# Two output projections in one slot, an earlier PSUM evacuation, and two low parts on GpSimd, in a fused attention and MLP block

## The chip, the cores and the metric

The kernel runs on one core of a Trainium2 chip. The metric is the device time of the program in microseconds (us). Times of a kernel are given as the median of several runs; the profile shows one execution, taken by the hardware profiler. The engines are called PE (TensorE; PEld its weight loads), DVE (VectorE), ACT (ScalarE), POOL (GpSimd) and SP (SyncE, which issues nearly all DMAs).

## The reference

A transformer block in float32 over 2048 rows of width 512. All the computing is in these lines:

```python
# attention on LayerNorm(x): 32 heads of 16, window of 8 positions with stride 2
qkv = layernorm(x) @ wqkv                      # 512 x 1536
logits = einsum("bhsd,bhswd->bhsw", q, k[idx]) * 16**-0.5   # idx = pos - 2*(0..7), masked below 0
o = einsum("bhsw,bhswd->bhsd", softmax(logits), v[idx])
h = x + o @ wo                                 # 512 x 512
# MLP on LayerNorm(h): 1792 hidden units, squared ReLU
r = relu(layernorm(h) @ w1 + b1)
out = h + (r * r) @ w2 + b2
```

## The kernel before

**Tiles.** The 2048 rows are 16 tiles of 128 rows, t = 0 to 15, and a block is R = 4 tiles (512 rows). Each matrix product keeps close to float32 precision by splitting each operand into a high part (a cast, `hi`, L152, always on ACT) and a low part (the difference, `lo`, L155, on DVE or POOL), and by summing three products: high by high, high by low, low by high. For one 128x512 result over a depth of 512 this is 12 matmuls (`mm3`, L228).

**Stages.** First the projections to q, k and v, whose results go through DRAM; then passages u = 0, 1, 2 (the text counts them 1, 2, 3), and then a last passage (4) of another form. The windowed attention (products on DVE at L340 and L351, sums on DVE at L374 and on POOL at L408) runs as a stream of steps beside all of it: `pump` emits as many of its DVE steps as a running estimate of PE's and DVE's time lets in.

**A passage u** has FB + LAG = 17 slots p = 0 to 16 and does three things at once on PE:

- `mlp1(u, f)` in slots 0 to 13: the first product of the MLP of block u, for hidden block f (128 hidden units x 512 rows), 12 matmuls into a PSUM bank. Its evacuation `hidden` (on ACT: bias and ReLU at L875, square at L876, cast to the high part `rh`; then the low part `rl` on POOL) is put with `at(1, ...)`, so it is emitted in the next slot.
- `mlp2(u, f)` in slots 3 to 16, three slots behind: the second product (L899), into four `acc` banks.
- For the four tiles t = 4(u + 1) + i of the next block: `wo_product` (attention output times `wo`, 12 matmuls into a bank), in the slots of the table `WP`: 9, 10, 13, 14 for passages 1 and 2. Behind it `h_add` (DVE adds `x` and takes the LayerNorm statistics), `h_norm` (three small POOL instructions for the factor, then ACT at L196), `add_b2` on POOL and `spill` (a store of `h` to DRAM), each so many slots after the product as the tuple in the call says.

**Turning.** An operand of a product must lie with its depth on the partitions, so o and the normalised h have to be transposed. Most tiles go through the DMA: ACT splits the float32 words into two 16-bit planes (`turn_split`, L621), SP issues a transposing DMA (`turn_dma`, L625), ACT joins the planes (`turn_join`, L630), and then high and low parts are made (`o_join`: `oh`, `ol`, or `ohl` for the third tile of a block; `h_parts`: into `big_l`, which also holds `hh` and `hl`, the operands of mlp1). The third and fourth tile of blocks 1 and 2 turn their h on PE instead (`h_T`, L201), in slot 16, ahead of and in the middle of that slot's second product.

**Order inside a slot.** `at(d, ...)` puts work into the list `due` of the slot d further on, `after` into `late`, `midway` into `amid`. A slot emits first the chores of its table entry (with `wo_product` last among them), then mlp1, then mlp2, and at its end `due`, the attention steps of `pump`, `amid` and `late`. Each engine runs its own instructions in the order in which they were emitted, and waits at the first one that is not ready. PE, ACT, DVE, POOL and SP are five such queues.

**Banks.** In the passages `turn["mm"]` and `turn["tr"]` are one turn over two banks, `mm1` and `mm0`: each mlp1, each `wo_product` and each `h_T` takes the other bank than the one before it in program order. It can be written only when the engine that reads its last content is done.

**The last passage** computes block 3's first product by a scheme with seven instead of eight quarter products. Its operands are sums of quarters of `hh`, made by `split_last` for tiles 12 to 15: for tiles 14 and 15 ACT casts, DVE forms the sums `s` (L757, L758, L766, L767), and low parts go into `big_l` (`hl` and `a_l[2]`) and `wo_l` (`a_l[1]`, `a_l[3]`, `a_l[4]`). `products_a` (L822) begins the passage on PE with the quarter products 1, 6, 5, 4; number 5 reads `a_h[1]` and `a_l[1]`, number 4 reads the third and fourth tile's part of `hh` and `hl`.

Of the kernel before, what the change touches and what calls it, by code (L numbers as in the profile page):

```python
# [19 lines left out]
R = 4  # L20
# [23 lines left out]
W2 = (18,)  # L44
LH = 3, 4, 10, 11
OP = 6, 7, 12, 13
WP = 9, 10, 13, 14
HP = 15, 15, 16, 16
UP = 14, 14, 15, 15
HL = (13, 0), (13, 1), (15, 0), (15, 1)  # L50
# [8 lines left out]
def block_kernel(ctx, tc, x, wqkv, wo, w1, b1, w2, b2, out):  # L59
    nc = tc.nc  # L60
# [52 lines left out]
    def at(delta, fn, *a):  # L113
        due.setdefault(now["slot"] + delta, []).append((fn, a))

    def after(delta, fn, *a):
        late.setdefault(now["slot"] + delta, []).append((fn, a))
# [33 lines left out]
    def hi(dst, src):  # L151
        nc.scalar.copy(dst, src)  # L152

    def lo(eng, dst, src, h):
        eng.tensor_tensor(out=dst, in0=src, in1=h, op=ALU.subtract)  # L155
# [53 lines left out]
    def hi_T(tr, h_dst):  # L209
        for d, src in parts(tr, h_dst):  # L210
            hi(d, src)
# [525 lines left out]
    def split_last(i, tr):  # L737
        hs_, ls_ = [a[:, :, i] for a in hh], [a[:, :, i] for a in hl]
        if i < RI:
            hi_T(tr, hs_)  # L740
            lo_T(tr, hs_, ls_)
            return
        j = i - RI
        tr0 = last_tr[j]
        if not j:
            a_h.update({2: hh[0][:, :, RI:], **{m: wo_h[:, m % 4].rearrange(
                "p (k i c) -> p k i c", k=2, i=RI) for m in (1, 3, 4)}})
            a_l.update({2: hl[0][:, :, RI:], **{m: wo_l[:, m % 4].rearrange(
                "p (k i c) -> p k i c", k=2, i=RI) for m in (1, 3, 4)}})
            for m in range(1, 5):  # L750
                s32[m] = row("s").rearrange("p (k i c) -> p k i c", k=2, i=RI)
        sm = {m: s32[m][:, :, j] for m in (1, 2)}
        sub, add = ALU.subtract, ALU.add
        tt = nc.vector.tensor_tensor
        a21 = tr[:, :2]
        hi(hs_[1], tr[:, 2:])
        tt(out=sm[1], in0=tr[:, 2:], in1=a21, op=add)  # L757
        tt(out=sm[2], in0=sm[1], in1=tr0[:, :2], op=sub)  # L758
        lo(nc.vector, ls_[1], tr[:, 2:], hs_[1])
        hi(a_h[2][:, :, j], sm[2])  # L760
        lo(nc.vector, a_l[2][:, :, j], sm[2], a_h[2][:, :, j])
        if not j:
            return
        hi(a_h[1], s32[1])
        for j in range(RI):
            tt(out=s32[3][:, :, j], in0=last_tr[j][:, :2], in1=last_tr[RI + j][:, :2], op=sub)  # L766
            tt(out=s32[4][:, :, j], in0=last_tr[j][:, 2:], in1=s32[2][:, :, j], op=sub)  # L767
        for m in (3, 4):
            hi(a_h[m], s32[m])
        for m in (1, 3):  # L770
            lo(nc.vector, a_l[m], s32[m], a_h[m])
# [97 lines left out]

    hid = {}  # L870

    def hidden(u, f, ps):
        r = row("r")
        rh, rl = work.tile([P, D], F32R, name="rh", bufs=LAG + 1), row("rl", dt=F32R)
        nc.scalar.activation(r, ps, AF.Relu, bias=b1_sb[:, f:f + 1])  # L875
        nc.scalar.activation(r, r, AF.Square)  # L876
        hi(rh, r)
        at(0, lo, nc.vector if u == R - 1 else nc.gpsimd, rl, r, rh)
        hid[u, f] = rh, rl

    def mlp1(u, f):
        ps = turn["mm"].tile("mm")
        fs = slice(f * P, (f + 1) * P)
        mm3(ps, lambda k: w1_h[:, k, fs], lambda k: w1_l[:, k, fs],
            lambda k: hh[k // 2][:, k % 2], lambda k: hl[k // 2][:, k % 2])
        at(1, hidden, u, f, ps)

    def mlp2(u, f, acc, js, first=False, last=False, mid=None):

# [91 lines left out]
    for n in range(16):  # L981
        gp, t = divmod(n, 4)
# [111 lines left out]
    for u in range(R - 1):  # L1094
        now["sub"] = u
        first, end = u == 0, False
        fs = list(range(FB)) if first else [*sorted(place), 12, 13]
# [8 lines left out]
        for i in js:  # L1106
            t = R * (u + 1) + i
            if not end:
                a = i // 2 if u == 2 else 0
                b = int(i == 1 and u < 2)  # L1110
                o0 = OP[i] - a - (2 if i >= RI and t in OV else 0) - (t == 15)
                if t in OV:
                    turned = [(o0 + a * (i == RI), after if i == RI and not a else at, 0, o_split, t),
                              (o0 + a * (i == RI), at if i > RI and u < 2 else after, i // (RI + 1) if u < 2 else 0, turn_dma, ("o", t)),
                              (o0 + 1, after, 0, o_join, t, 1) if i == RI and u == 1 else
                              (o0 + 2, at, 0, o_join, t)]
                else:
                    turned = [(o0, o_T, t)]
                if t in HV:
                    h0 = 11 + min(i, RI)  # L1120
                    turned += [(h0, at if t >= 14 else midway, 0, h_split, t), (h0, after, 0, turn_dma, ("h", t)),
                               (h0 + 2 - (t > 12), after if t > 12 else at, 0, turn_join, ("h", t))]
                for p, *what in ((LH[i] - a, at, 0, load_h, t), *turned,
                                 (WP[i] - a - (t == 15), wo_product, t, (0, 1, 2 + 3 * a + b + (t == 15), 3 + 3 * a + b + (t == 15)))):
                    todo.setdefault(p, []).append(what)
                p, h = (HP[i], i % 2) if u < 2 else HL[i]
                if t in HV:
                    todo.setdefault(p, []).append((after if t in (12, 13) else at, 0, h_parts, t))
                else:
                    (todo, halves)[h].setdefault(p, []).append((h_T, t))  # L1130
            todo.setdefault(UP[i], []).append((at, 0, unspill, R * u + i))
# [10 lines left out]
        for p in range(FB + LAG):  # L1142
            more = 0.0
            if p == FB:
                run(due)
                dve(HOLD)
            if u < 2 and p == FB - 2:
                dve(HOLD)
            for fn, *a in sorted(todo.get(p, []), key=lambda x: x[0] is wo_product):
                fn(*a)  # L1150
                more += 2.73 if fn is wo_product else 0.0
            if p < FB:
                mlp1(u, fs[p])
                more += 2.73
                if first:
                    after(0, split_w2, p)
                    if p + 1 < FB:
                        load_w2(p + 1)
            q = p - LAG
            if q >= 0:  # L1160
                f = fs[q]
                mlp2(u, f, acc, js, q == 0, q == FB - 1,
                     (lambda: half(p)) if p in halves else None)
                more += 2.74
                if f < 12 and (need or first and p < FB - LAG):
                    free.append(place.pop(f))
                    if need:
                        at(1, fetch, need.pop(0))
            end_slot(more)
# [5 lines left out]
    u = R - 1  # L1175
    now["sub"] = u
    fs = [f for pair_ in PAIRS for f in pair_]
# [45 lines left out]
    h = hs[S // P - 1]  # L1223
# [34 lines left out]
```

## Time and profile before

| | us |
|---|---|
| median of 3 runs | 504.54 (503.73 to 505.6) |
| the profiled execution | 504.29 |
| its span | 502.5 |
| PE busy | 496.0 (99%) |
| DVE, POOL, ACT busy | 381.6, 353.9, 301.6 |

The profiled execution's time is 1.8 us longer than its span. A row of the timeline gives the start (us from the span's start), the duration, the engine, the line, the operation, what it writes and reads, the shape, how many instructions the row stands for, and in brackets how long the engine had been idle before it and what it waited for. Rows of several instructions run from the start of the first to the end of the last; a PE row's duration includes the drain of its last matmul, so that the starts of neighbouring rows, and not the durations, give PE's pace.

### The profile page before, as it was taken

How to read it: one execution, taken by the hardware profiler on the slowest of the kernel's cores; microseconds unless marked ns; L12 is line 12 of the kernel's file. 1: busy time of each engine (PE TensorE's matmuls, PEld its weight loads, DVE VectorE, ACT ScalarE, POOL GpSimd, SP SyncE). 2: the span in 40 equal slices, each digit the busy share in tenths (PEclk: the TensorE clock that was granted, in tenths of full speed). 3: DMA queues.
4: the chain of work that ended last, by engine and by line, in shares of the span. 5: the costliest groups of instructions: out<-in, count | busy, mean ns of one | idle time of the engine just before them, and what ended most of it. 6: DMA issues, size and time to landing. Idle time of an engine off the chain costs nothing.

```text
span 502.5 us, 7519 instructions
## 1 busy us (share of the span) xinstructions
PE 496.0 (99%) x2414; PEld 420.5 (84%) x2414; DVE 381.6 (76%) x524; ACT 301.6 (60%) x540; POOL 353.9 (70%) x430
## 2 busy tenths in 40 slices
PE   8999999999999999999999999999999999999997
PEld 7999888888888888887888888888888888998986
DVE  6479899988989899988879998888974155833233
ACT  4635687668446758368564555755554958766541
POOL 5714898885685999869777877769799363786610
PEclk9999999999999999999999999999999999999999
DMA  9679979889698989589676756966654566355112
GB/s 280 184 221 243 294 234 316 254 291 282 201 226 255 299 283 257 182 239 224 195 253 209 211 150 193 232 213 237 211 160 66 128 165 188 112 162 167 64 42 86
DMA packets 111472, 103.15 MB, mean 205 GB/s; under 512 B 31560, under 2 KB 79944, under 8 KB 111432
## 3 DMA queue, kind: packets, MB, share of 16 engines
q1 hardware_dynamic: 110488, 102.14, 69.5%
q10 hardware_dynamic: 944, 0.52, 0.3%
q8 instruction: 19, 0.31, 0.3%
q14 instruction: 21, 0.17, 0.1%
HBM read 72.65 MB, written 24.25 MB: 193 GB/s over the span
## 4 chain that ended last, share of the span: by engine, by line
PE 80%; DVE 5%; POOL 4%; ACT 4%; DMA 3%; issue 3%; ACTq 0%; SPq 0%; DVEq 0%; POOLq 0%
PE mm L228 41%; PE acc L899 23%; PE wo L228 8%; PE mm L822 7%; PE tr L201 2%; POOL pr L408 1%; DVE pr L351 1%; DMA raw<-in_B_w_dram 1%; DMA o<-pl 1%; DMA wraw<-in_A_wqkv_dram 1%; POOL rl L155 1%; DVE ex L374 1%; DVE pr L340 1%; ACT pl L621 1%; ACT big_h L152 1%
## 5 line engine op out<-in xcount | busy, mean ns | idle before, releaser
L408 POOL TENSOR_TENSOR pr<-pr 128x512 f32<-128x512 f32 (+1 forms) x128 | 134.2, 1049 | 36.7 <-DVE pr L351 31.4
L228 PE MATMUL mm<-big_l,w_h 128*128 128x512 f32 x336 | 88.5, 390 | 0.0
L351 DVE TENSOR_TENSOR pr<-ex,v 128x1024 f32<-128x1024 f32 x64 | 78.0, 1220 | 12.2 <-POOL o L408 8.0
L340 DVE TENSOR_TENSOR pr<-qp,k 128x1024 f32<-128x1024 f32 x64 | 76.8, 1200 | 11.7 <-ACT qp L268 7.9
L374 DVE TENSOR_REDUCE ex<-pr 128x64 f32<-128x1024 f32 x64 | 78.5, 1226 | 2.0
L228 PEld LDWEIGHTS mm<-big_l,w_h 128*128 128x128 f32 x336 | 62.9, 188 | 13.5 <-ACT r L875 0.2
L155 POOL TENSOR_TENSOR rl<-r,rh 128x512 fp32r<-128x512 f32 x42 | 54.7, 1306 | 25.5 <-ACT rh L152 25.4
L228 PE MATMUL mm<-big_l,xh 128*128 128x512 f32 (+1 forms) x208 | 55.8, 378 | 0.0
L228 PE MATMUL mm<-big_h,xh 128*128 128x512 f32 (+1 forms) x208 | 53.6, 378 | 0.9 <-ACT xh L152 0.8
L228 PE MATMUL mm<-big_h,xl 128*128 128x512 f32 (+1 forms) x208 | 52.6, 374 | 0.0
L899 PE MATMUL acc<-big_h,rh 128*128 128x512 f32 x190 | 52.0, 391 | 0.0
L899 PE MATMUL acc<-big_l,rh 128*128 128x512 f32 x190 | 52.0, 390 | 0.0
L899 PE MATMUL acc<-big_h,rl 128*128 128x512 f32 x190 | 51.7, 389 | 0.0
L228 PE MATMUL mm<-big_l,w_l 128*128 128x512 f32 x168 | 44.9, 389 | 0.0
L228 PEld LDWEIGHTS mm<-big_h,xh 128*128 128x128 f32 x208 | 37.7, 188 | 7.8 <-ACT xh L152 2.0
L228 PEld LDWEIGHTS mm<-big_h,xl 128*128 128x128 f32 x208 | 38.2, 188 | 6.0 <-DVE xl L155 0.2
L899 PEld LDWEIGHTS acc<-big_h,rl 128*128 128x128 f32 x190 | 35.7, 188 | 7.4
L899 PEld LDWEIGHTS acc<-big_l,rh 128*128 128x128 f32 x190 | 35.6, 188 | 7.5
L228 PEld LDWEIGHTS mm<-big_l,xh 128*128 128x128 f32 x208 | 37.5, 188 | 4.9
L899 PEld LDWEIGHTS acc<-big_h,rh 128*128 128x128 f32 x190 | 35.0, 188 | 6.7
L875 ACT ACTIVATE r<-mm,b_sb 128x512 f32<-128x512 f32 x42 | 28.7, 684 | 14.0 <-PE mm L228 13.1
L228 PEld LDWEIGHTS mm<-big_l,w_l 128*128 128x128 f32 x168 | 31.5, 188 | 6.6
(160 smaller groups left out, 910.6 us busy)
## 6 DMA issues: line engine op xcount, KB each, us to landing
k<-qkv_d SPq DMA_DIRECT2D x48, 288.0 KB, 3.6
v<-qkv_d SPq DMA_DIRECT2D x48, 288.0 KB, 3.7
qkv_d<-y SPq DMA_DIRECT2D x18, 512.0 KB, 4.0
big_l<-w2l_d SPq DMA_DIRECT2D x24, 256.0 KB, 3.2
xt<-in_A_x_dram SPq DMA_DIRECT2D x16, 256.0 KB, 4.3
q<-qkv_d SPq DMA_DIRECT2D x32, 128.0 KB, 3.7
h<-in_A_x_dram SPq DMA_DIRECT2D x16, 256.0 KB, 3.6
h_d<-h SPq DMA_DIRECT2D x16, 256.0 KB, 2.8
```

The lines of the kernel that those rows point to most:

```text
L152: nc.scalar.copy(dst, src)
L155: eng.tensor_tensor(out=dst, in0=src, in1=h, op=ALU.subtract)
L201: nc.tensor.transpose(tr[:, k, :], src[:, k * P:(k + 1) * P], ident)
L228: nc.tensor.matmul(ps, l(k), r(k), start=(n == 0), stop=(n == 3 * KB - 1))
L340: nc.vector.tensor_tensor(out=pr.rearrange("p i w h d -> p i w (h d)"), in0=qps["now"][:, j % 2].unsqueeze(2).to_broadcast([P, RI, W, GC]) ...
L351: nc.vector.tensor_tensor(out=p2, in1=vwin, op=ALU.mult, in0=e1[:, :, :, j * GH:(j + 1) * GH].unsqueeze(4).to_broadcast([P, RI, W, GH, DH]))
L374: nc.vector.tensor_reduce(out=lf[:, :, :, j * GH:(j + 1) * GH], in_=pr, axis=X, op=ALU.add)
L408: nc.gpsimd.tensor_tensor(out=dst, in0=p2[:, :, :w], in1=p2[:, :, w:2 * w], op=ALU.add)
L621: nc.scalar.copy(two_planes(planes[key][1]), halves_of(src))
L822: nc.tensor.matmul(ps, sta[y][:, k], mov[x][:, k], start=(first and q == 0), stop=(last and q == len(terms) - 1), skip_group_check=True)
L875: nc.scalar.activation(r, ps, AF.Relu, bias=b1_sb[:, f:f + 1])
L899: nc.tensor.matmul(acc[j], l[:, j * P:(j + 1) * P], w[f], start=(first and n < len(js)), stop=(last and n >= len(terms) - len(js)))
```

## The change

Four edits:

1. `WP` gets a row for passages 1 and 2 and one for passage 3. In passages 1 and 2 the third tile's `wo_product` moves from slot 13 to slot 14, where the fourth tile's stands: PE then does mlp1 of the last hidden block and a second product first, and the two projections after each other. Passage 3 keeps its slots (9, 10, 12, 12).
2. The last hidden block of passages 1 and 2 is evacuated in its own slot (`after(0, hidden, ...)`) instead of the next.
3. The join of the first tile's h in passages 1 and 2 goes from `at` to `after`, so it is emitted behind the join of the fourth tile's o.
4. In `split_last` the low part of `hl` for tiles 14 and 15 is made by POOL instead of DVE.

```diff
-WP = 9, 10, 13, 14
+WP = (9, 10, 14, 14), (9, 10, 12, 12)
...
-        lo(nc.vector, ls_[1], tr[:, 2:], hs_[1])
+        lo(nc.gpsimd, ls_[1], tr[:, 2:], hs_[1])
...
-    def hidden(u, f, ps):
+    def hidden(u, f, ps, then=at):
...
-        at(0, lo, nc.vector if u == R - 1 else nc.gpsimd, rl, r, rh)
+        then(0, lo, nc.vector if u == R - 1 else nc.gpsimd, rl, r, rh)
         hid[u, f] = rh, rl
 
-    def mlp1(u, f):
+    def mlp1(u, f, last):
...
-        at(1, hidden, u, f, ps)
+        if u < 2 and f == last:
+            after(0, hidden, u, f, ps, after)
+        else:
+            at(1, hidden, u, f, ps)
...
-                               (h0 + 2 - (t > 12), after if t > 12 else at, 0, turn_join, ("h", t))]
+                               (h0 + 2 - (t > 12), after if t > 12 or not i and u < 2 else at, 0, turn_join, ("h", t))]
...
-                                 (WP[i] - a - (t == 15), wo_product, t, (0, 1, 2 + 3 * a + b + (t == 15), 3 + 3 * a + b + (t == 15)))):
+                                 (WP[u // 2][i], wo_product, t, (0, 1, 2 + 3 * a + b + (t == 15), 3 + 3 * a + b + (t == 15)))):
...
-                mlp1(u, fs[p])
+                mlp1(u, fs[p], fs[-1])
```

On ACT, passage 1, slots 13 and 14. `mm_2645` and `mm_2717` (after: `mm_2704`) are the first products of the last two hidden blocks, `r`, `rh` their evacuation, `pl<-o`, `oh` tile 7's attention output, `pl<-hn` tile 4's normalised h. Before:

```order
L875 ACTIVATE r_2742<-mm_2645,b1_sb_83 128x512
L876 ACTIVATE r_2742<-r_2742 128x512
L152 CAST rh_2743<-r_2742 128x512
L630 COPY pl_2626<-hn_2576 128x1024
L630 COPY pl_2619<-o_2104 128x1024
L152 CAST oh_2750<-pl_2619 128x512
L268 COPY qp_2767<-q_2634 128x256
L397 ACTIVATE ex_219<-ex_219 128x256
L152 CAST w2_x_1961<-raw2_2658 128x512
L875 ACTIVATE r_2790<-mm_2717,b1_sb_83 128x512
```

And now:

```order
L875 ACTIVATE r_2729<-mm_2645,b1_sb_83 128x512
L876 ACTIVATE r_2729<-r_2729 128x512
L152 CAST rh_2730<-r_2729 128x512
L630 COPY pl_2619<-o_2104 128x1024
L152 CAST oh_2736<-pl_2619 128x512
L268 COPY qp_2744<-q_2634 128x256
L630 COPY pl_2626<-hn_2576 128x1024
L875 ACTIVATE r_2757<-mm_2704,b1_sb_83 128x512
L876 ACTIVATE r_2757<-r_2757 128x512
L152 CAST rh_2758<-r_2757 128x512
L152 CAST w2_x_1961<-raw2_2658 128x512
```

The join of tile 4's h stands behind tile 7's, the last evacuation ahead of the cast of `w2_x` (the last block of w2), and the exponential `ex` of the attention behind both.

On DVE, the same place. `h<-wo,h` with the two statistics behind it is one tile's `h_add` (`h_2537` tile 6, `h_2617` tile 7), `big_l<-pl` are low parts of tiles 4 and 5, `big_l<-tr` of tiles 6 and 7. Before:

```order
L340 TENSOR_TENSOR pr_2782<-qp_2767,k_2632 128x1024
L155 TENSOR_TENSOR w2_x_1961<-raw2_2658,w2_x_1961 128x512
L666 TENSOR_TENSOR h_2617<-wo_2797,h_2617 128x512
L163 BN_STATS st_2828<-h_2617 128x6
L164 BN_AGGR mv_2829<-st_2828 128x2
L363 TENSOR_REDUCE sm_2781<-ex_219 128x32
L374 TENSOR_REDUCE ex_219<-pr_2782 128x16x4
L155 TENSOR_TENSOR big_l_85<-pl_2626,big_l_85 128x2x128 x2
L155 TENSOR_TENSOR big_l_85<-pl_2688,big_l_85 128x2x128 x2
L380 RECIPROCAL sm_2781<-sm_2781 128x32
L340 TENSOR_TENSOR pr_2867<-qp_2767,k_2693 128x1024
L155 TENSOR_TENSOR big_l_85<-tr_2873,big_l_85 128x2x128 x2
```

And now, from the same low part of `w2_x` on:

```order
L155 TENSOR_TENSOR w2_x_1961<-raw2_2658,w2_x_1961 128x512
L666 TENSOR_TENSOR h_2537<-wo_2766,h_2537 128x512
L163 BN_STATS st_2810<-h_2537 128x6
L164 BN_AGGR mv_2811<-st_2810 128x2
L666 TENSOR_TENSOR h_2617<-wo_2779,h_2617 128x512
L163 BN_STATS st_2816<-h_2617 128x6
L164 BN_AGGR mv_2817<-st_2816 128x2
L340 TENSOR_TENSOR pr_2830<-qp_2744,k_2632 128x1024
L363 TENSOR_REDUCE sm_2829<-ex_219 128x32
L374 TENSOR_REDUCE ex_219<-pr_2830 128x16x4
L155 TENSOR_TENSOR big_l_85<-pl_2626,big_l_85 128x2x128 x2
L155 TENSOR_TENSOR big_l_85<-pl_2688,big_l_85 128x2x128 x2
```

Tile 6's sum and statistics, which stood further ahead, and one L340 now stand behind the `w2_x` low part; the rows after these are as before.

On DVE and on POOL, ahead of the last passage (`pl_4530` is tile 14's turned h, `pl_4532` tile 15's). DVE:

```order
 L757 TENSOR_TENSOR s_4598<-pl_4530 128x2x128
 L758 TENSOR_TENSOR s_4599<-s_4598,pl_4396 128x2x128
-L155 TENSOR_TENSOR big_l_85<-pl_4530,big_l_85 128x2x128
 L155 TENSOR_TENSOR big_l_85<-s_4599,big_l_85 128x2x128
 L757 TENSOR_TENSOR s_4598<-pl_4532 128x2x128
 L758 TENSOR_TENSOR s_4599<-s_4598,pl_4482 128x2x128
-L155 TENSOR_TENSOR big_l_85<-pl_4532,big_l_85 128x2x128
 L155 TENSOR_TENSOR big_l_85<-s_4599,big_l_85 128x2x128
 L766 TENSOR_TENSOR s_4600<-pl_4396,pl_4530 128x2x128
```

POOL:

```order
 L155 TENSOR_TENSOR tl_4557<-traw_4459,th_4556 128x512 x2
 L155 TENSOR_TENSOR rl_4563<-r_4561,rh_4562 128x512
+L155 TENSOR_TENSOR big_l_85<-pl_4530,big_l_85 128x2x128
+L155 TENSOR_TENSOR big_l_85<-pl_4532,big_l_85 128x2x128
 L155 TENSOR_TENSOR tl_4683<-traw_4464,th_4682 128x512
 L850 TENSOR_TENSOR r_4706<-u_4653,p_4652 128x256
```

The two low parts have left DVE's row and stand on POOL between the low part of a hidden block and that of the second pair's weights.

## The prediction, made before the changed kernel was run

> **What bounds the kernel now.** I read the page's busy times first, then the waits of the PE alone, then the timeline around each wait.
>
> ```profile
> PE 496.0 (99%) x2414; PEld 420.5 (84%) x2414; DVE 381.6 (76%) x524; ACT 301.6 (60%) x540; POOL 353.9 (70%) x430
> ```
> ```profile
> PE tr L951 <- POOL ident masks.py:199: 1.3, 1, 1.3
> PE mm L228 <- ACT xh L152: 0.8, 1, 0.8
> PE wo L228 <- ACT ohl L152: 0.5, 1, 0.5
> PE mm L822 <- DVE wo_l L155: 0.5, 1, 0.5
> ```
>
> TensorE (PE) is busy for 496.0 of 502.5 us, and its whole list of waits has four rows. The first two belong to the warm-up transposes and the first projection. The other two are one wait each: for `ohl`, the high part of a turned attention output, and for `wo_l`, low parts of the fourth passage's operands. The change touches the neighbourhood of exactly these two, so no more is to be won here than they cost; everything else that it moves can only hurt, by making PE wait where it does not wait now. PE is the path that sets the end, so a microsecond of new wait is a microsecond of time unless a later wait swallows it, and behind the last row there is none.
>
> **Part 1: passage 1 (tiles 4 to 7; the third and fourth are 6 and 7).** PE around the wait:
>
> ```profile
> 227.34 1.07 PE L899 MATMUL acc<-big_h,rl 128*128 128x512 f32 x4
> ...
> 228.91 1.20 PE L228 MATMUL wo<-wo_h,ohl 128*128 128x512 f32 x4 [0.51 <-ACT ohl L152]
> ...
> 237.21 1.07 PE L228 MATMUL wo<-wo_h,oh 128*128 128x512 f32 x4
> ...
> 249.03 1.07 PE L228 MATMUL mm<-big_l,w_h 128*128 128x512 f32 x4
> ```
>
> Rows of four matmuls follow each other every 0.91 us when nothing holds them, so tile 6's product could have begun at 227.34 + 0.91 = 228.25; it began at 228.91, and its first four took 1.20 instead of 1.07. That is 0.66 + 0.13, about 0.8 us, and the change removes it: PE now has the passage's last first product (2.72 us) and a second product (2.72) to do ahead of tile 6, and `ohl` is there long before. **Term: -0.8.**
>
> What is late next? In the new order mlp1 of the last block, tile 6's and tile 7's products take banks in turn from two (`mm0`, `mm1`), with no other tile between them. So tile 7's product needs the bank that the last block's first product filled, and ScalarE (ACT) must have emptied it; before, tile 6's early product stood between them, and tile 7 took a bank that VectorE had emptied. That is why the evacuation is moved into its own slot. PE reaches tile 7 at 237.21 - 0.8 = 236.4. When does ACT get there?
>
> ```profile
> 232.14 1.17 ACT L630 COPY pl<-hn 128x1024 uint16<-128x1024 uint16 x1
> 233.60 1.17 ACT L630 COPY pl<-o 128x1024 uint16<-128x1024 uint16 x1 [0.30 <-DMA o<-pl]
> 234.81 0.62 ACT L152 CAST oh<-pl 128x512 fp32r<-128x512 f32 x1
> 235.34 0.37 ACT L268 COPY qp<-q 128x256 f32<-128x256 f32 x1
> 237.43 0.37 ACT L397 ACTIVATE ex<-ex 128x256 f32<-128x256 f32 x1 [1.72 <-DVE ex L393]
> 237.71 0.61 ACT L152 CAST w_x<-raw 128x512 fp32r<-128x512 f32 x1
> 238.22 0.69 ACT L875 ACTIVATE r<-mm,b_sb 128x512 f32<-128x512 f32 x1
> ...
> 239.61 0.63 ACT L152 CAST rh<-r 128x512 fp32r<-128x512 f32 x1
> ```
>
> The join of tile 7's output (L630, at 233.60) waits for its transposing DMA, whose place on SP's queue is not changed. Before, ACT filled that time with the join of `hn` (232.14); the change puts that join behind, so ACT now idles from 232.2 to 233.6 and does the join afterwards: qp at 235.34 as before, join of `hn` at 235.34 + 0.28 (the step from 237.43 to 237.71) = 235.62, then `r` at about 235.62 + 1.1 = 236.7, done at 236.7 + 0.68 = 237.4. PE, ready at 236.4, waits 1.0 and restarts like the old wait with 0.13 more. **Term: +1.1**, between 0 (if the DMA lands a microsecond earlier) and 1.3 (if it lands a little later).
>
> Next, VectorE (DVE). Its rows behind this point:
>
> ```profile
> 239.57 0.67 DVE L155 TENSOR_TENSOR w_x<-raw,w_x 128x512 fp32r<-128x512 f32 x1
> 240.17 0.68 DVE L666 TENSOR_TENSOR h<-wo,h 128x512 f32<-128x512 f32 x1
> ...
> 241.71 0.39 DVE L363 TENSOR_REDUCE sm<-ex 128x32 f32<-128x256 f32 x1
> ...
> 245.50 1.15 DVE L340 TENSOR_TENSOR pr<-qp,k 128x1024 f32<-128x1024 f32 x1
> 246.86 0.76 DVE L155 TENSOR_TENSOR big_l<-tr,big_l 128x256 fp32r<-128x256 f32 x2 [0.21 <-ACT big_l L152]
> ```
>
> The pair at 246.86 reads tile 6's transposes out of the bank that the next passage's first product writes at 249.03; now it is done 1.4 us before. In the new order there stands between the `w_x` low part and this pair, besides what stood there, tile 6's sum and statistics (240.17 to 241.71 for tile 7: 1.54) and one L340 (1.15). And `w_x` can start only when ACT has cast its high part, now behind `r`: 236.7 + 1.39 (238.22 to 239.61) + 0.63 + 0.61 = 239.3. So the pair starts at 239.3 + (246.65 - 239.57 = 7.1) + 1.54 + 1.15 = 249.1 and ends at 249.8. PE arrives at 249.03 - 0.8 + 1.1 = 249.3. **Term: +0.4**, between 0 and 0.9 (0.5 more if a GpSimd instruction holds `w_x` up; part 3 shows such a case). Tile 6's and tile 7's statistics end at 239.3 + 0.67 + 1.54 = 241.5 and 243.0; PE transposes the two tiles ahead of and in the middle of the passage's last second product, 3.6 and 1.8 us before 249.3, which leaves GpSimd and ACT over 4 us for each: no cost. On SP's queue tile 6's store of `h` falls behind four loads of earlier `h` rows, and these now stand ahead of a `k` and a `q`; nothing that PE reads in this passage is among them: no cost.
>
> **Part 2: passage 2 (tiles 8 to 11).** No wait to remove. The same bank is wanted at 325.19:
>
> ```profile
> 321.35 1.17 ACT L630 COPY pl<-o 128x1024 uint16<-128x1024 uint16 x1
> ...
> 323.07 0.37 ACT L268 COPY qp<-q 128x256 f32<-128x256 f32 x1
> ...
> 325.19 1.07 PE L228 MATMUL wo<-wo_h,oh 128*128 128x512 f32 x4
> ```
>
> By the same steps: 323.07 + 0.28 + 1.1 + 0.68 = 325.1, a hair before PE. **Term: 0**, up to 0.3; if the DMA is earlier than its join here, there is a microsecond to spare.
>
> **Part 3: the two low parts, ahead of passage 4.**
>
> ```profile
> 420.81 1.29 POOL L155 TENSOR_TENSOR rl<-r,rh 128x512 fp32r<-128x512 f32 x1
> ...
> 421.28 1.10 DVE L757 TENSOR_TENSOR s<-pl 128x256 f32<-128x256 f32 x1 [3.52 <-POOL tl L155]
> ...
> 422.49 0.43 DVE L758 TENSOR_TENSOR s<-s,pl 128x256 f32<-128x256 f32 x1
> 422.83 0.42 DVE L155 TENSOR_TENSOR big_l<-pl,big_l 128x256 fp32r<-128x256 f32 x1
> ...
> 423.39 0.43 DVE L155 TENSOR_TENSOR big_l<-s,big_l 128x256 fp32r<-128x256 f32 x1
> ...
> 424.52 0.42 DVE L155 TENSOR_TENSOR big_l<-pl,big_l 128x256 fp32r<-128x256 f32 x1
> 424.64 0.41 ACT L152 CAST big_l<-s 128x256 fp32r<-128x256 f32 x1 [0.98 <-DVE s L758]
> ...
> 425.08 0.42 DVE L155 TENSOR_TENSOR big_l<-s,big_l 128x256 fp32r<-128x256 f32 x1
> ...
> 426.77 1.28 DVE L155 TENSOR_TENSOR wo_l<-s,wo_h 128x512 fp32r<-128x512 f32 x2
> 427.50 0.51 PE L822 MATMUL mm<-wo_l,th 128*128 128x256 f32 x2 [0.47 <-DVE wo_l L155]
> ```
> ```profile
> L408 POOL TENSOR_TENSOR pr<-pr 128x256 f32<-128x256 f32 x64 | 49.5, 774 | 5.0
> ```
>
> The rows at 422.83 and 424.52 leave DVE: 0.84 us of work. But each lies in a gap. The row behind the second, at 425.08, needs ACT's cast of `s` (424.64 to 425.05), and that waited for L758, not for the row that goes; at 422.83 it is the same. Without them DVE waits for ACT in that time. **Term: 0** from the removal, and PE's 0.5 to 0.6 at 427.50 stays.
>
> GpSimd is done with its own work at 422.1, but two instructions of about 0.77 us (the rate of the last row, same shape) are laid beside DVE work that reads SBUF twice, and that costs: the DVE row at 421.28 took 1.10 instead of 0.42, and ended at 422.38, 0.28 after the GpSimd row of 420.81 did. The Trainium skill (SBUF — State Buffer, section SBUF: two separate sides) calls the port pair of these engines an exclusive lock: of a DVE instruction with two SBUF inputs and a GpSimd instruction that reads SBUF, the one that starts first keeps it for its whole length and the other stands still. The row agrees. By that rule with both instructions in the chain's way the sum would end at the upper bound below, and by free overlap this term would be 0.
>
> By the rows: the first GpSimd instruction starts when L758 of tile 14 is done (422.9) and ends at 423.7, and DVE's 423.39 waits 0.3; the second comes ready then and, if it gets in between two DVE rows, delays the chain by another 0.77; if it falls into DVE's wait for ACT, by little. So 0 to 1.1; I take the middle, **+0.5**. Only DVE's chain to `wo_l` feels it; the moved low parts themselves are the last operands of the last of the four products with which passage 4 begins, and come in time.
>
> **Sum:** -0.8 + 1.1 + 0.4 + 0 + 0.5 = +1.2. The profiled execution took 504.29 (span 502.5 and 1.8 around it) and gives 505.5; it lay 0.25 below the median of 504.54, so I forecast 504.54 + 1.2 = 505.7. A measurement of this kernel tells about 0.5% (2.5 us) from no change, so this counts as no change.
>
> **Rivals.** *A: it works as meant.* The DMA lands early enough that tile 7 finds its bank empty, and DVE, with two rows fewer, reaches `wo_l` earlier. For it: PE has 5.4 us (six rows of 0.91) more before tile 6, and passage 2 shows a join that needed no wait. Against it: the 0.30 wait for the DMA at 233.60, and the gaps at 422.83 and 424.52. It gives -0.8 - 0.6 = -1.4: 503.1.
>
> *B: slower, by DVE's backlog.* DVE enters passage 2 some 2.6 us late (7.1 + 1.54 + 1.15 from 239.3, against 246.65) and does not catch up, since it has hardly any idle time there:
>
> ```profile
> 265.00:280.00 15.00, 15.00 (x68) 12.43 (x67) 14.01 (x16) 6.88 (x12) 11.85 (x14) 1.00 0.70 215
> 280.00:295.00 15.00, 15.00 (x68) 12.43 (x67) 14.06 (x19) 9.80 (x15) 12.05 (x15) 1.00 0.73 203
> ...
> 297.81 0.68 DVE L155 TENSOR_TENSOR ol<-pl,oh 128x512 fp32r<-128x512 f32 x1
> ...
> 299.81 1.07 PE L228 MATMUL wo<-wo_h,ol 128*128 128x512 f32 x4
> ```
>
> DVE (third engine column) is busy 14.0 of 15 us. Tile 9's low part ends at 298.5, PE wants it at 299.81: a lag of more than 1.3 us against PE decides for this case. At 2.6 us PE waits 1.3 there; with 0.9 at 249, 1.3 for the bank and 0.5 in part 3 that is -0.8 + 1.3 + 0.9 + 1.3 + 0.5 = +3.2: 507.7. Against it: PE is itself 0.7 later by then, and 1 us of 15 is idle.
>
> *C: nothing changes,* the new bank wait just equals the old wait, and the port costs nothing: 504.5.
>
> **How the numbers follow.** Forecast 0.50, A 0.27, B 0.11, C 0.12. The forecast's own terms span -0.8 + (0 to 1.3) + (0 to 0.9) + (0 to 0.3) + (0 to 1.1), 503.7 to 507.3; the range takes in A at the lower end: 502.9 to 507.2. Faster by over 0.5% (under 502.0) needs more than both waits are worth: 0.03. Slower by over 0.5% (over 507.1) is most of B: 0.08. The rest, 0.89, is within.
>
> **What would show it.** Right: no PE wait for `ohl`; a PE wait of about 1 us at tile 7's product for ACT's `r` (L875 in passage 1), with `hn`'s join between; a shorter one at passage 2's first product for DVE's `big_l<-tr`; in part 3, DVE rows of 0.7 or more beside GpSimd's two, and PE's wait for `wo_l` longer than 0.5. Wrong: tile 7's product starting by 236.5 without a wait breaks the first term; `wo_l` ready before 427.4 on the same clock (PE's start of passage 4 taken as zero) breaks part 3; a PE wait for `ol` at tile 9 makes it B.

## The result, and the profile after

The changed kernel takes 510.46 us (median of 6 runs, 508.7 to 512.09) against 504.39 of the kernel before (six runs too), a ratio of 1.0113 [1.009, 1.0137]: slower by 1.1%, above the forecast of 505.7 and its range of 502.9 to 507.2. A second set of six beside other runs gave 510.01, ratio 1.01 [1.0078, 1.0122]. The profiled execution took 510.56 (span 508.7).

The whole list of PE's waits in the profile after (us in total, times, longest):

```profile
PE mm L228 <- DVE big_l L155: 2.9, 1, 2.9
PE tr L954 <- POOL ident masks.py:199: 1.3, 1, 1.3
PE wo L228 <- ACT r L875: 1.2, 1, 1.2
PE mm L822 <- DVE wo_l L155: 0.9, 1, 0.9
PE mm L228 <- ACT xh L152: 0.7, 1, 0.7
PE tr L201 <- DVE xt L459: 0.4, 1, 0.4
```

The wait for `ohl` is gone, as meant. Two waits in the changed part are new, for `big_l` and for `r`, and the one for `wo_l` has grown by 0.4. The wait for `xt` (0.4) lies in the projections, which the change does not touch; it comes and goes between profiles (edit 4 alone has none). First the largest. PE's timeline at the boundary of passages 1 and 2:

```profile
247.84 1.09 PE L902 MATMUL acc<-w_x,rl 128*128 128x512 f32 x4
251.87 1.99 PE L228 MATMUL mm<-big_l,w_h 128*128 128x512 f32 x4 [2.94 <-DVE big_l L155]
253.66 1.86 PE L228 MATMUL mm<-big_l,w_l 128*128 128x512 f32 x4
255.36 2.00 PE L228 MATMUL mm<-big_l,w_h 128*128 128x512 f32 x8
257.20 1.07 PE L228 MATMUL mm<-big_l,w_l 128*128 128x512 f32 x4
```

and the busy time by stretch there (PE is the first pair of columns, the granted clock stands before the last two):

```profile
248.00:252.00 4.00, 1.06 (x5) 0.56 (x5) 4.00 (x8) 0.22 (x1) 1.11 (x1) 0.99 0.35 127
252.00:256.00 4.00, 4.00 (x11) 3.15 (x12) 3.91 (x8) 0.00 (x0) 0.00 (x0) 0.58 0.47 120
256.00:260.00 4.00, 4.00 (x19) 3.27 (x19) 2.77 (x4) 2.97 (x6) 1.43 (x2) 1.00 1.02 392
```

PE could have begun at 248.75 (247.84 and a row of 0.91), and begins at 251.87: the pause costs 3.1. Then the clock is granted at about half: by their starts eight matmuls fill 251.87 to 255.36, 3.5 us, and the next eight 255.36 to 257.20, 1.8. So the slow clock costs 1.7 more. That is 4.8 of the 6.2 by which the spans differ.

PE waits here for the bank that tile 6's transposes (`tr`) filled and that DVE must have read. Why is DVE late with it? These are its rows and GpSimd's in the profile before. DVE:

```profile
243.28 2.04 DVE L155 TENSOR_TENSOR big_l<-pl,big_l 128x256 fp32r<-128x256 f32 x4
245.24 0.34 DVE L380 RECIPROCAL sm<-sm 128x32 f32<-128x32 f32 x1
245.50 1.15 DVE L340 TENSOR_TENSOR pr<-qp,k 128x1024 f32<-128x1024 f32 x1
```

GpSimd, the additions of b2 to the rows of tiles 5, 6 and 7:

```profile
245.41 3.79 POOL L679 TENSOR_TENSOR h<-h,b_sb 128x512 f32<-128x512 f32 x3
```

After, DVE:

```profile
238.63 1.36 DVE L155 TENSOR_TENSOR w_x<-raw,w_x 128x512 fp32r<-128x512 f32 x1 [2.15 <-ACT w_x L152]
...
242.89 0.18 DVE L164 BATCH_NORM_AGGREGATE mv<-st 128x2 f32<-128x6 f32 x1
242.99 1.19 DVE L340 TENSOR_TENSOR pr<-qp,k 128x1024 f32<-128x1024 f32 x1
244.09 0.41 DVE L363 TENSOR_REDUCE sm<-ex 128x32 f32<-128x256 f32 x1
244.54 1.23 DVE L374 TENSOR_REDUCE ex<-pr 128x64 f32<-128x1024 f32 x1
245.68 4.05 DVE L155 TENSOR_TENSOR big_l<-pl,big_l 128x256 fp32r<-128x256 f32 x4
...
249.91 1.16 DVE L340 TENSOR_TENSOR pr<-qp,k 128x1024 f32<-128x1024 f32 x1
```

and GpSimd:

```profile
243.78 0.22 POOL L169 TENSOR_SCALAR rs<-mv 128x1 f32<-128x1 f32 x1
...
244.96 4.14 POOL L679 TENSOR_TENSOR h<-h,b_sb 128x512 f32<-128x512 f32 x3
```

Before, DVE's four low parts of tiles 4 and 5 (`big_l<-pl`) were done at 245.32, just ahead of the first addition. Now they start 0.72 behind it and take 4.05 instead of 2.04. One by one they take 0.86, 1.50, 1.50 and 0.41: three of the four wait in turn for one of the three additions. With L340 behind them the pair that frees the bank comes at 250.99 instead of the 249.1 of the forecast. This agrees with the exclusive lock that the prediction quoted from the Trainium skill (SBUF — State Buffer, section SBUF: two separate sides) for part 3. The prediction reckoned with a GpSimd instruction in DVE's way in part 3, and as a possible 0.5 more at `w_x`, but not here.

The second new wait is in passage 2. ACT there:

```profile
324.30 0.62 ACT L152 CAST rh<-r 128x512 fp32r<-128x512 f32 x1
327.24 1.18 ACT L630 COPY pl<-o 128x1024 uint16<-128x1024 uint16 x1 [2.32 <-DMA o<-pl]
...
329.29 1.16 ACT L630 COPY pl<-hn 128x1024 uint16<-128x1024 uint16 x1
```

The join of tile 11's `o` starts 6.09 us after its transposing DMA was issued (at 321.15; before it started 4.74 after the issue), the join of `hn` follows, and then `r`. PE starts tile 11's product at 331.09 instead of 329.7, and slowly: 1.5 with the restart.

In passage 1 the same bank costs little; PE's row there, whose four matmuls could have begun at 236.73:

```profile
236.81 1.20 PE L228 MATMUL wo<-wo_h,oh 128*128 128x512 f32 x4
```

Part 3, GpSimd's second low part and the DVE row beside it:

```profile
429.57 1.00 POOL L155 TENSOR_TENSOR big_l<-pl,big_l 128x256 fp32r<-128x256 f32 x1 [0.22 <-ACT big_l L152]
```
```profile
430.02 0.84 DVE L758 TENSOR_TENSOR s<-s,pl 128x256 f32<-128x256 f32 x1
```

L758 takes 0.84 instead of 0.42 and ends 0.29 after the GpSimd row.

### The profile page after: what moved, and what is told of

Its sections match the earlier page's. It is cut to its first block, busy times and chain, and to the rows that moved or that the text cites. A ratio compares the mean times of both kernels' runs of the same rounds, so it can differ in the third digit from the quotient of the medians.

```text
span 508.7 us, 7511 instructions
## 1 busy us (share of the span) xinstructions
PE 498.0 (98%) x2414; PEld 421.9 (83%) x2414; DVE 382.1 (75%) x522; ACT 301.9 (59%) x540; POOL 356.4 (70%) x432
## 4 chain that ended last, share of the span: by engine, by line
PE 40%; POOL 3%; ACT 2%; DVE 2%; issue 2%; DMA 1%; SPq 0%; POOLq 0%; DVEq 0%; ACTq 0%
PE acc L902 17%; PE mm L228 12%; PE mm L822 7%; PE wo L228 3%; DMA o<-pl 1%; POOL pr L408 1%; ACT pl L630 1%; ACT pl L621 1%; POOL tl L155 1%; POOL rl L155 1%; POOL o L408 0%; ACT r L875 0%; DVE s L757 0%; PE half L925 0%; DVE s L758 0%
## 5 line engine op out<-in xcount | busy, mean ns | idle before, releaser
L340 DVE TENSOR_TENSOR pr<-qp,k 128x1024 f32<-128x1024 f32 x64 | 76.8, 1200 | 10.8 <-ACT qp L268 9.0
L374 DVE TENSOR_REDUCE ex<-pr 128x64 f32<-128x1024 f32 x64 | 78.5, 1227 | 2.0
```

The costliest lines, as they stand in the source:

```text
L340: nc.vector.tensor_tensor(out=pr.rearrange("p i w h d -> p i w (h d)"), in0=qps["now"][:, j % 2].unsqueeze(2).to_broadcast([P, RI, W, GC]) ...
L374: nc.vector.tensor_reduce(out=lf[:, :, :, j * GH:(j + 1) * GH], in_=pr, axis=X, op=ALU.add)
```

## The experiments

Each ratio is against runs of the kernel before on the same chip. Edits are numbered as above: 1 the slot of the product, 2 the evacuation in its own slot, 3 the order of the joins, 4 the low parts on GpSimd.

### Which part costs what

Edits 1 to 3 in passage 1 alone:

```diff
-WP = (9, 10, 14, 14), (9, 10, 12, 12)
+WP = (9, 10, 14, 14), (9, 10, 13, 14), (9, 10, 12, 12)
...
```

(In a diff `...` stands for lines left out; here they confine edits 2 and 3 to the same passage and undo edit 4.)

> The change in passage 1 alone (tiles 4 to 7); passage 2 keeps slots 13 and 14, and the two low parts stay on DVE. Theory 1 (DVE comes late to tile 6's low parts at the end of passage 1, and PE waits there and restarts slowly): the wait of 2.9 us for DVE's big_l stands as in the changed kernel, the granted clock is below 1 behind it, and the time is 508 to 510 us. Rival (passages 1 and 2 and the low parts each cost a like share of the 6 us): 506 to 506.5.

509.25 (ratio 1.0083 [1.0054, 1.0112]). Edits 1 to 3 in passage 2 alone:

```diff
-WP = (9, 10, 14, 14), (9, 10, 12, 12)
+WP = (9, 10, 13, 14), (9, 10, 14, 14), (9, 10, 12, 12)
...
```

> The change in passage 2 alone. Theory 1: PE waits about 1.3 us for ACT's r at tile 11's product, and the old wait of 0.5 for ohl in passage 1 is back: 505.7. Rival (that wait is only a consequence of passage 1's lateness, which delays the transposing DMA): no wait there, 504.4.

506.14 (1.0037 [1.0021, 1.0054]). Edit 4 alone:

```diff
-        lo(nc.vector, ls_[1], tr[:, 2:], hs_[1])
+        lo(nc.gpsimd, ls_[1], tr[:, 2:], hs_[1])
```

> Edit 4 alone, the kernel before with the two low parts on POOL. Theory 1: PE's wait for wo_l grows from 0.5 to 0.9 us, because POOL's two instructions hold up DVE's chain; time 504.8, which can't be told from 504.4. Rival (it relieves DVE): the wait for wo_l shrinks below 0.5.

505.09 (1.0015 [0.9999, 1.0031]); PE's wait for `wo_l` is 0.9 instead of 0.5. So passage 1 carries most of the loss, passage 2 some 1.9 by itself, and the low parts 0.4 by PE's wait (the ratio's interval reaches down to no change). The first theory of each holds in the main; in passage 2 alone PE's wait for `r` is 0.8 instead of its 1.3. Of PE's waits with passage 1 alone these two are new:

```profile
PE mm L228 <- DVE big_l L155: 2.4, 1, 2.4
PE wo L228 <- ACT r L875: 1.6, 1, 1.6
```

### Is it GpSimd's additions?

The additions and the stores behind them put off by three to five slots:

```diff
-            (at if fn is h_add or fn is h_norm and t >= 14 else after)(n + (fn is add_b2), fn, *a)
+            (at if fn is h_add or fn is h_norm and t >= 14 else after)(n + (fn is add_b2) + (5 - 2 * (t > 5)) * (t in (5, 6, 7) and fn in (add_b2, spill)), fn, *a)
```

> The changed kernel with the additions of b2 (POOL, L679) and the stores behind them for tiles 5, 6 and 7 put 3 to 5 slots later, so that POOL is not busy while DVE makes the low parts of tiles 4 and 5 (245.7 to 249.7 us in the changed kernel). Theory 1a (DVE is late because these POOL instructions hold its SBUF reads): the four low parts take 1.4 to 2 us instead of 4.0, PE waits about 1 us instead of 2.9, the clock stays at 1.0, and the time falls by 3 to 4 us to about 507. Theory 1b (the order on DVE alone makes it late): the four low parts still take about 4 us and the time stays within 1 us of 510.5.

512.9 (1.0167 [1.0148, 1.0187]): slower still. At the end of passage 1 DVE's row is short,

```profile
247.53 1.42 DVE L155 TENSOR_TENSOR big_l<-pl,big_l 128x256 fp32r<-128x256 f32 x4
```

and PE's wait for `big_l` is gone. But a longer wait came in passage 2. SyncE, whose queue is worked off in order, stood at the stores for 22.1 us in all (12.5 in the changed kernel), with attention's loads behind them: a load of `q` was issued at 276.18 instead of 272.45, ACT waited 9.3 for it, and tile 9's `oh` came late. SyncE's waits and PE's:

```profile
SPq L682 <- POOL h L679: 22.1, 8, 5.9
```
```profile
PE wo L228 <- ACT oh L152: 3.5, 1, 3.5
```

The clean test leaves the three additions out and moves no other instruction (these rows lack b2, and their stores wait for less):

```diff
     def add_b2(t):
+        if t in (5, 6, 7):
+            return
```

> The changed kernel with GpSimd's three additions of b2 to the rows of tiles 5, 6 and 7 left out (these rows lack b2 in the output); everything else stands as in the changed kernel, and the stores of these rows now wait for less. Theory A (the additions hold DVE's four low parts of tiles 4 and 5 back, one for one): the four take 1.6 to 2.0 us instead of 4.0, TensorE's wait for the tr bank falls from 2.9 to between 0.4 and 1.0, no slice behind it is at half clock; the passage 2 wait of 1.2 for r stays. Time 510.5 - 2.2 - 1.5 = 506.8, between 506 and 507.5. Rival B (DVE was late by its own queue of work, the additions only lie beside it): the wait stays at 2.5 or more, time 510.

506.86 (1.005 [1.003, 1.0069]). The four low parts, smallest, median and largest of one in ns, and PE's waits:

```profile
L155 DVE TENSOR_TENSOR big_l<-pl,big_l x4: 415/418/418, 246.6 to 247.6; 128x256 fp32r<-128x256 f32 x4
```
```profile
PE wo L228 <- ACT r L877: 1.5, 2, 0.8
PE tr L956 <- POOL ident masks.py:199: 1.3, 1, 1.3
PE mm L824 <- DVE wo_l L155: 0.9, 1, 0.9
```

No wait for `big_l` in the list, a mean clock of 1.000, 3.2 us (by the ratios) less than the changed kernel. The boundary still costs 0.4: PE's first matmul of passage 2 starts at 250.17, where it could have at 249.88, and restarts slowly. Theory A is borne out; the four low parts are even shorter than it gave. That not all of the 4.8 comes back is in part the wait for `r` in passage 1, 0.8 here instead of 0.2.

### What does a pause cost?

The kernel before, with tile 6's pair of low parts written over and over (the same values) so that DVE comes late, four times and, in the second kernel, nine times:

```diff
+        for n in range(2 * 4 * (t == 6)):
+            at(0, lo, nc.vector, parts(tr, ls_)[n % 2][0], parts(tr, ls_)[n % 2][1], hs_[n % 2])
```

> The kernel before with DVE made late on purpose: at the end of passage 1 the two low parts of tile 6 are written four times more (the same values, eight instructions of about 0.33 us, 2.6 us in all), so that the pair that frees the tr bank for passage 2's first product ends about 250.3 instead of before 248.0, and TensorE, which arrives at 249.0, waits about 1.2 us. Theory A (a short pause costs its length, a pause of 3 us costs its length and then some us at half clock): time 504.2 + 1.3 = 505.5, granted clock of the slice behind the pause 0.95 to 1.00. Rival B (a pause costs its length whatever it is): the same 505.5. Rival C (the loss seen in the changed kernel came from elsewhere and this wait is absorbed later): within 0.3 of before, 504.3.

505.85, against 504.64: +1.2 (1.0031 [1.0013, 1.0048]) for this wait, at full clock:

```profile
251.70 1.15 PE L228 MATMUL mm<-big_l,w_h 128*128 128x512 f32 x4 [1.20 <-DVE big_l L155]
...
255.41 1.07 PE L228 MATMUL mm<-big_l,w_l 128*128 128x512 f32 x4
```

> As the run above with nine repeats (18 instructions, about 6.0 us of DVE): the pair ends about 253.7, TensorE waits about 4.6 us. Theory A: 4.6 for the pause and 1.5 to 2.0 more for half clock in the 3 to 4 us behind it: 504.2 + 6.3 = 510.5, with a slice behind the pause at a granted clock of 0.5 to 0.6. Rival B: 504.2 + 4.6 = 508.8, clock 1.0 behind the pause. Rival C: 504.3.

511.32, against 504.64: +6.7 (1.0136 [1.0112, 1.016]):

```profile
253.54 1.98 PE L228 MATMUL mm<-big_l,w_h 128*128 128x512 f32 x4 [4.53 <-DVE big_l L155]
...
258.88 1.07 PE L228 MATMUL mm<-big_l,w_l 128*128 128x512 f32 x4
```

Sixteen matmuls separate the two rows of each fence: 3.7 us behind the short pause, 5.3 behind the long one. So the half clock costs 1.6, and theory A holds against B. Three of the four executions with the long pause have a mean clock of 0.990 to 0.993, lower than the 0.997 of the one in the fence, so the +6.7 of the median holds more half clock than that.

### Which edit lets the additions in?

The changed kernel with edit 3 undone:

```diff
-                               (h0 + 2 - (t > 12), after if t > 12 or not i and u < 2 else at, 0, turn_join, ("h", t))]
+                               (h0 + 2 - (t > 12), after if t > 12 else at, 0, turn_join, ("h", t))]
```

> The changed kernel with one edit undone in passages 1 and 2: ACT joins hn ahead of o again, as in the kernel before, so that r of the first product's last block stands three rows nearer behind the join of o. Theory A (the bank waits come from the join of hn that the change put ahead of r, and passage 2's late landing comes with that order): both waits of TensorE for r go (0.2 in passage 1, 1.2 in passage 2), passage 2's join of o starts at most 4.8 us after its transposing DMA is issued; the wait for the tr bank of about 2.9 and its half clock stay: 510.5 - 1.5 = 509.0. Rival B (the landing is late because of what else is in flight, not because of ACT's order): the join of o still starts 5.6 to 6.1 us after the issue, but r still comes 1.5 us earlier and the wait for it is at most 0.3: 509.0 as well; only the start of the join tells A from B. Rival C (the bank is late whatever the order of the joins, since the output product of the second tile holds it): the wait in passage 2 stays at 1.0 or more, 510.5.

504.61 (1.0011 [0.9994, 1.0028]), 4.4 less than the nearest theory had it. Ten of twelve executions lay at 503.6 to 505.5, one at 507.85, one at 510.57, and that last one was the profiled one, with a wait for `big_l` of 3.0. Both waits for `r` were gone. The same kernel again, for a profile of its usual execution:

> The changed kernel with the joins in the old order a second time, for a profile of its usual execution (ten of its twelve came to 503.6 to 505.5, and the one profiled was the slowest, 510.6). Theory A (in the usual execution DVE's four low parts of tiles 4 and 5 do not lie beside GpSimd's three additions): the four take 1.4 to 2.0 us, the wait for big_l is under 0.6, no slice behind it below a clock of 0.9; 504 to 505. Rival B (they lie beside them always, and the usual execution is fast for another reason, a different stretch of attention): the four take 3.5 to 4.0, and the time is still below 506.

505.03, and no wait for `big_l`. DVE and then GpSimd in this one:

```profile
238.88 0.69 DVE L155 TENSOR_TENSOR w_x<-raw,w_x 128x512 fp32r<-128x512 f32 x1 [0.19 <-ACT w_x L152]
...
245.27 1.42 DVE L155 TENSOR_TENSOR big_l<-pl,big_l 128x256 fp32r<-128x256 f32 x4
```
```profile
246.37 3.97 POOL L679 TENSOR_TENSOR h<-h,b_sb 128x512 f32<-128x512 f32 x3
```

and DVE in the unlucky one:

```profile
239.53 1.78 DVE L155 TENSOR_TENSOR w_x<-raw,w_x 128x512 fp32r<-128x512 f32 x1 [0.36 <-ACT w_x L152]
```

where `w_x` started 0.65 later and was held for 1.1 us beside a GpSimd instruction; the first addition started at 246.29 and the first low part at 247.01. It is a race. Both sides start from tile 7's statistics: DVE goes by L340, L363 and L374 to its low parts, 2.8 us in the changed kernel (242.89 to 245.68), GpSimd by three small instructions to the additions, 2.1 (242.89 to 244.96, though it could begin only at 243.78). GpSimd wins unless its own work ahead holds it up, as in the usual execution, where it could begin only at 244.75. Each trace in which it won by 0.72 (the changed kernel twice, passage 1 alone, the unlucky execution) has 4.05 or 4.06 for the low parts. In the ten traces in which DVE led by 1.1 to 2.1 they take 1.4 to 2.0.

Edits 1 and 2 in passage 1 alone, with the old joins; edits 1 and 2 in passage 2 alone; edit 3 alone (the diffs are those above):

> The change in passage 1 alone, low parts on DVE, the joins in the order of the kernel before (b2 stays where it was). Theory A (the order of the joins decides whether DVE is late at the end of passage 1, since with the old order most executions of the whole change came to 504.6): 504.1 - 0.8 + 0 to 0.4 = 503.3 to 503.7, ratio 0.998 to 0.999, profile without a wait for big_l of over 0.5. Rival B (the old order only makes the lateness rarer by chance, passage 2's move or the low parts having a share in it): more than a third of the executions above 507, median 505 to 509.

504.14 (1.0 [0.9983, 1.0017]), three of twelve at 506.0 to 506.5, none above. No wait is left in passage 1, yet the median shows no gain; theory A had 0.4 to 0.8.

> The change in passage 2 alone, low parts on DVE, and the joins in the order of the kernel before: what is left is the move of tile 10's output product into tile 11's slot and the last block's own evacuation. Theory A: no wait for r in passage 2, and none of the other waits of the kernel before is touched: 504.3, ratio 0.998 to 1.001. Rival C (the bank is late whatever the order of the joins): a wait of 0.8 or more stays, 505.5 to 506, as with the changed order of the joins (506.1).

504.21 (1.0006 [0.9995, 1.0017]); no wait for `r`.

> The kernel before with one edit of the change alone: in passages 1 and 2 ACT joins o ahead of hn. No output product and no evacuation moves. Theory A (the join order makes DVE's low parts of tiles 4 and 5 fall beside GpSimd's additions): a wait for big_l at the start of passage 2, 506 to 509. Rival B (the join order is harmful only together with the move of tile 6's product, which takes the slack from ACT and DVE in the next slot): no wait for big_l over 0.3, 504.0 to 504.8, ohl's wait of 0.5 still there; a wait for r can come in passage 2 of at most 0.8.

504.34 (1.0001 [0.9988, 1.0014]): B, except that the wait for `ohl` was not there either. The order of the joins harms only together with the moved product.

Beside these, the changed kernel once more:

> The changed kernel as it is, beside the runs above on the same chip, to see whether it has the same two kinds of execution as the one with the old joins. Theory A (its DVE is late in every execution): all executions above 508, median 510. Rival B (it is late by chance, in some executions only): some executions at 504 to 507.

All six at 508.89 to 510.57: A. Last, the changed kernel with the one ACT instruction for which DVE stood 2.15 us, the cast of `w_x`, moved ahead of the join of `hn` and of `r`:

```diff
-                    after(0, split_w2, p)
+                    if p == 13:
+                        late[now["slot"]].insert(0, (split_w2, (p,)))
+                    else:
+                        after(0, split_w2, p)
```

> The changed kernel with one instruction of ACT moved: the cast of w_x in passage 1's last slots, for which DVE stood 2.15 us, goes ahead of the join of hn and of r; the order on DVE, GpSimd, SyncE and TensorE is that of the changed kernel. Theory A (the changed order of the joins harms because DVE stands at this cast while GpSimd runs on to its additions of b2, so that GpSimd has the lead where it used to be behind): DVE's four low parts start before the first addition and take 1.4 to 2.0, no wait for big_l over 0.4, no half clock; r comes 0.6 later than in the changed kernel, so a wait for it of 0.5 to 1.3 in passage 1, and 1.2 in passage 2 stays: 510.2 - 4.8 + 0.6 = 506.0, between 505.3 and 506.8. Rival B (the additions lead for another reason, GpSimd's own earlier work): the four low parts still take 3.5 to 4.0, the wait for big_l is 2 or more, 509 to 511.

508.96 (1.0071 [1.0048, 1.0094]), neither A nor B: four of ten executions at 506.0 to 507.6, six at 508.8 to 510.7. The profiled one, 510.25, shows why, DVE and then GpSimd:

```profile
245.21 4.72 DVE L155 TENSOR_TENSOR big_l<-pl,big_l 128x256 fp32r<-128x256 f32 x4
```
```profile
245.26 4.38 POOL L679 TENSOR_TENSOR h<-h,b_sb 128x512 f32<-128x512 f32 x3
```

A dead heat: GpSimd's lead fell from 0.72 to -0.05, and the executions part. So DVE's wait for the cast is a share of the reason. The rest is not shown: GpSimd's `rl` also comes earlier (241.08 in the changed kernel, 242.04 in the usual execution with the old joins), but no run moves it alone.

### Two tries for a faster kernel

On the kernel before, passage 1's second product in slot 13 (`down`, the lines that stood there as a function) ahead of tile 6's product and of mlp1:

```diff
...
+            now_first = u == 0 and p == 13
+            if now_first:
+                down()
...
-                mlp2(u, f, acc, js, q == 0, q == FB - 1,
-                     (lambda: half(p)) if p in halves else None)
+                if not now_first:
+                    down()
```

> Not a part of the change: the kernel before, with only the order on TensorE of one slot of passage 1 altered, where tile 6's output product waits 0.5 us for its high parts ohl. The second product of that slot, whose operands have long been ready, goes ahead of the output product; slots, banks, GpSimd and DVE work stand where they stood. Theory A (the wait goes and nothing takes its place, since no bank changes hands in another order): 504.2 - 0.5 to 0.8 = 503.5, no wait for ohl. Rival B (the output product ends 2.7 us later, so its addition, its normalisation and the transposes of tile 6 come later and DVE is late at the passage boundary, as in the changed kernel): a wait for big_l of 0.5 to 2 us, 505 to 506.

505.75 (1.0019 [1.0002, 1.0035]). The wait for `ohl` is gone, as theory A has it, but the time is rival B's; the new wait is not the one it named, but one at PE's next product:

```profile
PE wo L228 <- DVE ol L155: 1.1, 1, 1.1
```

And edits 1 and 2 in passage 1 with the old joins and the three additions moved behind the sums at the start of passage 3:

```diff
...
+        if t in LB:
+            nc.gpsimd.tensor_tensor(out=h, in0=h, in1=b2_sb, op=ALU.add)
+            after(1, nc.sync.dma_start, out_v[b, e, i], h)
```

> What is left of the change when the three causes found are taken out: passage 1's move alone, the joins in the order of before, low parts on DVE, and b2 of tiles 5, 6 and 7 added on GpSimd after the second product's sum, at the start of passage 3, instead of beside DVE's low parts at the end of passage 1 (the output is complete; these rows' stores to the outputs wait one slot longer). Theory A (with the causes out, only the gain that the change is built on is left): no wait for ohl, none over 0.4 for big_l or r in passage 1, 504.4 - 0.5 to 0.8 = 503.7. Rival B (DVE's queue at the end of passage 1 is full even without the additions): a wait for big_l or ol of 0.5 to 1.0 is left, 504.4, no difference from before. Rival C (the additions put at the start of passage 3 hold DVE there in the same way): a new wait of 1 us or more after 345 us, 505.5.

506.34 (1.0049 [1.0036, 1.0062]): passage 1 and its boundary have no wait, but passage 3 has three new ones (`oh` 0.5, `ol` 0.5, `r` 0.3), nearest to rival C, whose one wait of 1 us or more did not come. No version beat the kernel before by more than can be measured.

## Why the prediction was wrong, point by point

**The step that failed** is the one that ended in "Term: +0.4, between 0 and 0.9", the bank that DVE must free for passage 2's first product. Its mechanism was right and its size was not: the boundary cost 4.8. The sum carried the four low parts of tiles 4 and 5 at the 2.04 that they took before, and did not ask what GpSimd does in the place they were moved to. The rows were at hand: 243.28 + 2.04 ends 0.09 ahead of 245.41, where the additions begin. The wait came to 3.1: some 0.5 as forecast, 2.0 from the lock (4.05 instead of 2.04), and the rest because PE came at 248.75 instead of 249.3, having waited less in passage 1. With the additions left out the boundary costs 0.4, the forecast's term. And a pause of that length has a second price, half clock, 1.6 to 1.7, that the prediction had nowhere.

That the low parts started where the sum has them (239.3 + 3.71 + 1.54 + 1.15 = 245.70, measured 245.68) was luck: `w_x` started 0.67 earlier than forecast, at 238.63, and took 0.69 longer beside a GpSimd instruction.

**The bank in passage 1, +1.1:** 0.2 in the profile after (a second profile has 0.3, others 0.7 to 1.6, the last above the range). The mechanism is the one forecast, and the size changes from profile to profile.

**Passage 2, "Term: 0, up to 0.3":** 1.5. The step took the old start of the join for the landing. In all nine traces with the product moved in passage 2 the join starts 5.4 to 6.1 us after the issue, with the new joins and the old; in the nine without the move it starts within 4.76. With the old joins the late landing costs PE nothing (504.21). A transposing DMA reports its end in sixteen parts. In six of the nine traces fifteen parts report 3.7 to 4.6 us after the issue, as without the move, and one reports 1.5 later; in the other three all sixteen are late. What holds them up stays open; the loads issued around it are the same.

**The wait for `ohl`, -0.8:** gone in every kernel with the move in passage 1. But it is no sure gain. Of the seven profiles whose passage 1 has the old slots and the old order on PE, three have the wait (0.5 to 0.6: the kernel before and twice passage 2 alone); in the other four (edit 3 alone, edit 4 alone, both pauses) it is 0.1 at most. PE comes to that place 0.4 to 1.9 us later in these four than in the profile before, by time lost ahead of passage 1; but passage 2 alone came 1.1 later and still waited, so that is not all. The forecast took one profile's wait for the kernel's. That agrees with the 504.14 of passage 1 with the old joins.

**Part 3, +0.5:** +0.4, and by the forecast's mechanism: the second GpSimd instruction got in ahead of a DVE row of the chain.

**The rivals.** A and C are out by the time. B had DVE late, but for another reason (two rows more in its queue) and at another place: there is no wait for `ol` at tile 9. Its 2.6 us is also 2.4 by its own rows (239.3 + 7.1 + 1.54 + 1.15 - 246.65). Summed by the rows of the two profiles: -0.8 + 0.2 + 3.1 + 1.7 + 1.5 + 0.4 = +6.1, of the 6.2 between their spans.

## What to carry to other kernels

Before moving a run of VectorE instructions with two SBUF inputs, look at what GpSimd does in the place they move to, not only at VectorE's own queue: a lead of 0.7 us decided over 3 to 6 us here. Price a new wait of TensorE of 2 us and more at its length plus the half clock behind it, 1.6 to 1.7 here. Look at several profiles before counting a wait of half a microsecond as a gain. When a bundle of edits loses, undo them one by one: one edit here, harmless alone, carried nearly the whole loss in company.

## What the runs showed of the hardware that was not expected

- VectorE and GpSimd took turns: four DVE instructions of 0.42 beside three GpSimd ones of 1.29 took 4.05 to 4.72 together, and the GpSimd ones behind the first 1.47 each. DVE instructions in a row did not keep GpSimd out: in the trace of the moved cast DVE's first started 0.05 ahead, and its second took 1.51.
- Half clock came behind each pause of 2.04 to 4.53 us (seven profiles) and, past the first 20 us of the program, behind none of up to 1.60. By the traces' record of the clock it lasted 3.41 us each time and began 0.1 to 1.4 us after TensorE had resumed; it cost 1.6 to 1.7. The Trainium skill (TensorE: Matmul & The Clock Gate, section Part 1: The HAM clock gate) has it behind an idle window of about 3.4 us; here a wait of 2.04 was enough in the trace of the moved cast:

```profile
252.07 1.17 PE L228 MATMUL mm<-big_l,w_h 128*128 128x512 f32 x4 [2.04 <-DVE big_l L155]
```
```profile
254.00:256.00 2.00, 2.00 (x6) 1.60 (x5) 2.00 (x5) 0.00 (x0) 0.00 (x0) 0.50 0.32 83
```

- Half clock is not the same in every execution: of the second set of the changed kernel four have a mean clock of 0.996 or 0.997 (509.8 to 510.6) and two of 0.999 and 1.000 (508.9).
